# Attention's row maxima subtracted by PE in PSUM, one exp per step, and stage 2's x tile laid over x2

## The chip, the cores and the metric

The kernel runs on one core of a Trainium2 chip. The metric is the device time of one execution in microseconds (us). Engines: PE (TensorE, with its weight loads as PEld), DVE (VectorE), ACT (ScalarE), POOL (GpSimd), SP (SyncE, here a queue of DMA issues).

## What is computed

Three layers run one after the other: attention with banded masks, a mixture of experts whose tokens are assigned one expert each, and a second mixture in which every token goes through all eight experts and the results are weighed by a Sinkhorn-normalised matrix.

```python
def _attn_ref(q, k, v):                      # (4, 8, 576, 64) each
    scores = scale * np.matmul(q, k.transpose(0, 1, 3, 2))
    scores = np.where(masks[None], scores, -1e9)
    scores = scores - np.max(scores, axis=-1, keepdims=True)
    attn = np.exp(scores)
    attn = attn / (np.sum(attn, axis=-1, keepdims=True) + 1e-09)
    return np.matmul(attn, v)
...
    # _moe_ref: one expert per token, 288 tokens per expert
    h = np.maximum(x[mask] @ w1[e], 0.0)
    out[mask] = h @ w2[e]
...
    # _moe2_ref: P from 8 Sinkhorn rounds, every token through every expert
    out += P[:, e:e + 1] * (np.maximum(x @ w1[e], 0.0) @ w2[e])
```

## The kernel before

Each engine takes its instructions in the order in which they are written (the schedule is manual); semaphores join the engines. Three parts matter here.

**Attention** (`attention`, lines 99 to 366). The 4 batches are cut into 6 blocks of 96 queries with 128 keys each. A *unit* has 8 heads: 4 heads of the plain mask (kind 0) and 4 of the dilated one (kind 1, its tokens reordered so that the mask is a band too), one block apart. There are 25 units; the first and the last have one kind only, so half the work. A unit goes through these helpers:

- `scores` (line 163): PE adds the masks as a bf16 product with an identity (line 169, 256 columns, four of them) and Q times K in f32 (line 176, eight products of 128 columns with 64 rows each) into one PSUM tile `ps_s` of two banks; there are two such tiles.
- `row_max` (line 179): DVE reduces `ps_s` to a maximum per row and head (`nm`, line 182), ACT scales it by -1/8 (line 183).
- `exps` (line 186): ACT takes exp of one head at a time, 8 instructions of 128 columns, with the maximum as a bias (line 192). It is a generator: after 4 heads it gives way to `x_out`.
- `p_trans` (line 195): PE transposes the 8 blocks in f32 into `ps_p`, of which there is one.
- `p_evac` (line 203): DVE copies them to SBUF (`pt`, line 207).
- `pv` (line 209): PE multiplies by V (line 218) into `ps_v`, of which there is one; DVE divides by the sums (lines 224 to 226). For some steps PE also makes the router's logits of finished tiles there (line 288) or turns a block (line 258).
- `x_out` (line 237): ACT and POOL split the result into two f16 halves (lines 240, 241), SP stores them.

The loop (line 303) runs 27 iterations. Iteration n writes `scores` and `row_max` of unit n, `p_trans` and `p_evac` of n-1, the exps of n around `x_out` of n-3, and `pv` of n-2. From iteration 4 on, `next(side)` adds half a weight piece of the second mixture's first expert: one ACT instruction (line 742) and one DVE instruction (line 744). `FILL` puts four 512-column products of zeros into iteration 0.

**Stage 1** (`Moe.stage1`) runs routing and the first mixture, and the second mixture's expert 0. It ends with `m2_l1(8)` (line 848, which reads the activations `x2` and the weights `w0h`, `w0l`) and `m2_l2(8)` (line 936), beside the Sinkhorn rounds (lines 1259 to 1270, whose PE product is line 1265: `mean` times `P`, f32, 144 columns).

**Stage 2** (`Moe.stage2`) runs experts 1 to 7 in blocks of 384 tokens. `x_load` (line 1051) brings a block's activations (`xb`, two DMAs of 1344 KB, one buffer), `s_l1` (line 1120) and `s_l2` (line 1158) are its matmuls. Its three SBUF pools are opened in the order `n_t`, `n_x` (the tile `xb`), `n_h`, and lie from address 135200 of a partition upwards, where stage 1's right-hand pools lay until then: `x2h` 137760 to 156192, `x2l` to 174624, the first layer's weights `w0h`, `w0l` to 191008, the second layer's weights to 207392. With this order `xb` lies at 164384 to 185888, over the end of `x2l`, `w0h` and part of `w0l`. The first DMA into it waits for the PE count that the last matmul of line 936 in `m2_l2(8)` brings. Six warming products of 512 columns (line 757) follow `x_load(0)` on PE.

Of the kernel before, what the change touches and what calls it, by code (L numbers as in the profile page):

```python
# [11 lines left out]
F32 = mybir.dt.float32  # L12
F16 = mybir.dt.float16
BF = mybir.dt.bfloat16
I32 = mybir.dt.int32
AF = mybir.ActivationFunctionType
OP = mybir.AluOpType
# [6 lines left out]
QB = 96  # L24
# [7 lines left out]
SC = 0.125  # L32
# [49 lines left out]
NU = len(UNITS)  # L82
# [29 lines left out]
def attention(tc, q, k, v, masks, wg, ident, xd, L, zero, side, early, keep, tables):  # L112

    nc = tc.nc
    with ExitStack() as ctx:
        one = ctx.enter_context(tc.tile_pool(name="a_one", bufs=1))
        ld = ctx.enter_context(tc.tile_pool(name="a_ld", bufs=2))
        vp = ctx.enter_context(tc.tile_pool(name="a_v", bufs=3))
        wk = ctx.enter_context(tc.tile_pool(name="a_w", bufs=2))
        ps = ctx.enter_context(tc.tile_pool(name="a_ps", bufs=2, space=bass.MemoryType.PSUM))  # L120

        raw, T, VR, SS, PP, PT, XT = {}, {}, {}, {}, {}, {}, {}
# [9 lines left out]
        def part(u, size):  # L132

            ks = list(UNITS[u])
            return slice(ks[0] * size // 2, (ks[-1] + 1) * size // 2)

        idf = one.tile([128, 128], F32)
        idb = one.tile([QB, QB], BF)
        idh = one.tile([QB, QB], F16)
        mk = one.tile([QB, MASKS.shape[1], 2, 128], BF)  # L140
        wgf = one.tile([128, 4, E], F32)
        wgh = one.tile([128, 4, E], F16)
# [15 lines left out]
        def op_ap(nm, h, b, j):  # L158
            pair, s = divmod(h, 2)
            p0, n = (max(QB * j - 32, 0), 128) if nm == "k" else (QB * j, QB)  # L160
            return raw[nm, b, pair // 2][64 * s:64 * s + 64, pair % 2, p0:p0 + n]

        def scores(u):
            p = SS[u] = ps.tile([QB, 2, 4, 128], F32, name="ps_s")
            kinds = UNITS[u]
            gs = part(u, 4)
            for s in range(2):
                for n, (kind, (b, j)) in enumerate(kinds.items()):
                    nc.tensor.matmul(p[:, s, 2 * kind:2 * kind + 2, :], idb,
                                     mk[:, MASK_ID[j], kind:kind + 1, :].to_broadcast([QB, 2, 128]),  # L170
                                     start=(n == 0), stop=False, skip_group_check=True)
            for g in range(gs.start, gs.stop):
                for s in range(2):
                    h = 2 * g + s
                    b, j = kinds[g // 2]
                    nc.tensor.matmul(p[:, s, g, :], op_ap("q", h, b, j), op_ap("k", h, b, j), start=False,  # L176
                                     stop=(g + 1 == gs.stop), skip_group_check=True)

        def row_max(u):
            p, gs = SS[u], part(u, 4)  # L180
            nm = wk.tile([QB, 2, 4], F32, name="nm")
            nc.vector.tensor_reduce(nm[:, :, gs], p[:, :, gs], axis=AX.X, op=OP.max)
            nc.scalar.activation(nm[:, :, gs], nm[:, :, gs], AF.Copy, scale=-SC)
            PP[u] = nm

        def exps(u):
            p, nm, gs = SS.pop(u), PP[u], part(u, 4)
            e = wk.tile([QB, 2, 4, 128], F32, name="e")
            PP[u] = e
            for s in range(2):  # L190
                for g in range(gs.start, gs.stop):
                    nc.scalar.activation(e[:, s, g, :], p[:, s, g, :], AF.Exp, bias=nm[:, s, g:g + 1], scale=SC)
                yield

        def p_trans(u):
            e, gs = PP.pop(u), part(u, 4)
            p = ps.tile([128, 2, 512], F32, name="ps_p", bufs=1)
            for s in range(2):
                for g in range(gs.start, gs.stop):
                    nc.tensor.transpose(p[:, s, g * QB:(g + 1) * QB], e[:, s, g, :], idf[:QB, :QB])  # L200
            return p

        def p_evac(u, p):
            gs = part(u, 4)
            t = PT[u] = wk.tile([128, 2, 4, QB], F32, name="pt")
            pp = p[:, :, :4 * QB].rearrange("p s (g q) -> p s g q", g=4)
            nc.vector.tensor_copy(t[:, :, gs], pp[:, :, gs])

        def pv(u, extra, turn=None):
            t = PT.pop(u)  # L210
# [69 lines left out]
        def logits(p, c):  # L280
# [9 lines left out]
            return lambda: nc.vector.tensor_copy(L[:, c, :], p)  # L290

        warm(18)
        nc.vector.tensor_copy(idb, idf[:QB, :QB])
        nc.vector.tensor_copy(idh, idf[:QB, :QB])
        loaded = []
        for kind in (1, 0):
            for nm in "kq":
# [2 lines left out]
            load_v(1, kind)  # L300
        xl = [one.tile([128, 2, 2, S], F16, name="xl%d" % kind) for kind in range(2)]
        first = S * (B - 1) // 128
        for n in range(NU + 2):
            if n < NU:
                scores(n)
                row_max(n)
            if 1 <= n <= NU:
                p_evac(n - 1, p_trans(n - 1))
            ex = exps(n) if n < NU else iter(())
            next(ex, None)  # L310
            if 3 <= n <= NU:
                x_out(n - 3)
            for _ in ex:
                pass
            if n == NU:
                early()
            if n in FILL:
                warm(FILL[n])
            if n >= 2:
                pv(n - 2, [loaded.pop(0)[1] for _ in range(1 if n < NU else 3) if loaded and loaded[0][0] <= n],  # L320
                   n - 3 if NU - 4 <= n <= NU else None)
            if n == 1:
                nc.gpsimd.dma_start(wgf, wg)
                tables()
            elif n == 4:
                nc.scalar.activation(wgh, wgf, AF.Copy, scale=SG)
                nc.vector.scalar_tensor_tensor(wgl, wgf, SG, wgh, op0=OP.mult, op1=OP.subtract)
            if 4 <= n:
                next(side, None)
            if n == 9:  # L330
                tables(True)
            b, c = divmod(n - NJ - 2, NJ)
            if 0 <= b < B - 2 and c < 2:
                load_v(b + 2, 1 - c)
            b, c = divmod(n - NJ, NJ)
            if 0 <= b < B - 2 and c < 2:
                for nm in "kq":
                    load_qk(nm, b + 2, 1 - c)
            b, c = divmod(n - 10, NJ)
            if 0 <= b < B - 1 and c < 3:  # L340
                c0, c1 = S * b // 128, S * (b + 1) // 128
                c0, c1 = c0 + 2 * c, min(c0 + 2 * c + 2, c1)
                if c1 > c0:
                    x_load(c0, c1)
                    loaded += [(n + 3, i) for i in range(c0, c1)]
            if n == NU - 1:
                x_load(first, first + 1)
            if n == NU:
                loaded += [(n, i) for i in (first, first + 1)]
# [5 lines left out]
        p = ps.tile([128, 2, 512], F32, name="ps_v", bufs=1)  # L355
# [311 lines left out]
class Moe:  # L667
# [82 lines left out]
    def psum(self):  # L750
        return self.ps.tile([128, 512], F32, name="mm", bufs=6)

    def warm(self, n):

        p = self.psum()
        for _ in range(n):
            self.nc.tensor.matmul(p, self.zero[:, :128], self.zero, start=True, stop=True)

    def weights(self, key, fetch):

# [608 lines left out]
    def stage2(self, ctx):  # L1369


        pool = lambda n, b: ctx.enter_context(self.tc.tile_pool(name=n, bufs=b))
        self.tp, self.bp, self.hp = pool("n_t", 1), pool("n_x", 1), pool("n_h", 1)

        def part():
            lo = self.tp.tile([128, 2, 2, BLK], F32, name="r", bufs=2).bitcast(F16).rearrange(
                "p a b m -> p (a b m)")[:, :7 * 256].rearrange("p (k c) -> p k c", k=7)
            return self.tp.tile([128, 3, BLK], F32, name="S", bufs=1)[:, :, :256], lo

        def l1(e, n, b):  # L1380
            for j, ns in enumerate(self.s_l1(b)):
                if n and e + 1 < E and j in (0, 1, 3):
                    next(new)
                yield ns

        self.x_load(0)
        for _ in range(6):
            self.warm(1)
        for e in range(1, E):
            order = list(range(NB))[::1 if e % 2 else -1]  # L1390
            new = self.staged(e + 1, part) if e + 1 < E else iter(())
            for n, b in enumerate(order):
                if n == 0:
                    next(new, None)
                interleave(l1(e, n, b), self.side if (e, n) == (1, 0) else None)
                if n + 1 < NB:
                    self.x_load(order[n + 1])
                elif e + 1 < E:
                    self.last_piece()
                    self.w_load(0)  # L1400
                for j, _ in enumerate(self.s_l2(e)):
                    if j in (8, 10, 16, 20, 23, 43):
                        next(new, None)
                if n + 1 == NB:
                    for _ in new:
                        pass
                    if e + 1 < E:
                        self.w_load(1)
# [45 lines left out]
```

## Time and profile before

| what | us |
|---|---|
| three runs | 1804.84, 1805.51, 1808.44 (median 1805.51) |
| the profiled execution, its own time | 1803.2 |
| its span | 1801.4 |
| PE busy | 1738.0 (96% of the span) |
| DVE busy | 1359.0 (75%) |
| ACT busy | 852.7 (47%) |
| POOL busy | 239.6 (13%) |
| mean granted clock of TensorE | 0.982 of full speed |

The span is what the profile records; the execution's own time has 1.8 us around it. Attention takes about the first 115 us, stage 1 lasts until about 629 us, stage 2 until the end. "Busy" on PE is modelled, since matmuls are pipelined: an instruction's duration includes its way through the array, so the pace of a stream is read from the starts, or from the chain of waits, where consecutive pieces stand end to end.

### The profile page before, as it was taken

How to read it: one execution, taken by the hardware profiler on the slowest of the kernel's cores; microseconds unless marked ns; L12 is line 12 of the kernel's file. 1: busy time of each engine (PE TensorE's matmuls, PEld its weight loads, DVE VectorE, ACT ScalarE, POOL GpSimd, SP SyncE). 2: the span in 40 equal slices, each digit the busy share in tenths (PEclk: the TensorE clock that was granted, in tenths of full speed). 3: DMA queues.
4: the chain of work that ended last, by engine and by line, in shares of the span. 5: the costliest groups of instructions: out<-in, count | busy, mean ns of one | idle time of the engine just before them, and what ended most of it. 6: DMA issues, size and time to landing. Idle time of an engine off the chain costs nothing.

```text
span 1801.4 us, 35276 instructions
## 1 busy us (share of the span) xinstructions
PE 1738.0 (96%) x14464; PEld 1290.0 (72%) x14464; DVE 1359.0 (75%) x2583; ACT 852.7 (47%) x1581; POOL 239.6 (13%) x297
## 2 busy tenths in 40 slices
PE   9986899999999989999999999999999999999998
PEld 7864676667776657777777777777777777777776
DVE  6977785678744858878887888788788878887556
ACT  5853442343443345555554456444455544464433
POOL 2423331223320000000000000000000000000111
PEclk9977999999999999999999999999999999999999
DMA  8923441424442132445225443424452254433020
GB/s 295 288 65 108 121 121 61 131 78 121 143 139 67 57 130 98 170 154 201 114 89 206 159 150 133 162 101 170 157 197 116 90 202 159 150 134 154 36 97 36
DMA packets 105554, 241.20 MB, mean 134 GB/s; under 512 B 46192, under 2 KB 69888, under 8 KB 98480
## 3 DMA queue, kind: packets, MB, share of 16 engines
q1 hardware_dynamic: 84592, 151.27, 24.3%
q0 software_dynamic: 20544, 87.42, 13.8%
q8 instruction: 113, 1.85, 0.4%
q14 instruction: 49, 0.40, 0.1%
q10 hardware_dynamic: 256, 0.26, 0.0%
HBM read 173.63 MB, written 61.73 MB: 131 GB/s over the span
## 4 chain that ended last, share of the span: by engine, by line
PE 72%; DVE 11%; issue 10%; ACT 4%; DMA 2%; POOL 1%; SPq 0%; POOLq 0%; ACTq 0%; DVEq 0%
PE mm L1120 27%; PE mm L1158 23%; PE mm L848 8%; PE mm L936 5%; PE mm L892 2%; PE r L542 1%; PE ps_v L218 1%; DVE hl L1077 1%; PE ps_p L200 1%; PE ps_s L176 1%; POOL out_dram L1172 1%; DVE G L488 1%; DVE w1l L789 1%; DVE G L615 1%; ACT w1h L788 1%
## 5 line engine op out<-in xcount | busy, mean ns | idle before, releaser
L1120 PE MATMUL mm<-xb,w1h 128*128 128x384 f16 x2352 | 574.8, 327 | 7.8 <-issue 4.8
L1158 PE MATMUL mm<-w2h,hh 128*128 128x256 f16 x1764 | 480.8, 273 | 0.4
L1158 PE MATMUL mm<-w2h,hl 128*128 128x256 f16 x1764 | 480.8, 273 | 0.0
L1158 PE MATMUL mm<-w2l,hh 128*128 128x256 f16 x1764 | 480.8, 273 | 0.0
L1120 PE MATMUL mm<-xb,w1l 128*128 128x384 f16 x1176 | 383.9, 326 | 0.0
L1158 PEld LDWEIGHTS <-hh 128*128 128x128 f16 x3528 | 345.2, 98 | 43.1 <-issue 0.9
L1120 PEld LDWEIGHTS <-w1h 128*128 128x128 f16 x2352 | 230.3, 98 | 159.5 <-issue 11.4
L1158 PEld LDWEIGHTS <-hl 128*128 128x128 f16 x1764 | 172.6, 98 | 19.9
L1077 DVE TENSOR_TENSOR hl<-r,hh 128x1536 f16<-128x1536 f32 x84 | 147.5, 1756 | 42.7 <-ACT hh L1076 42.7
L1120 PEld LDWEIGHTS <-w1l 128*128 128x128 f16 x1176 | 115.2, 98 | 79.3 <-issue 3.5
L1072 ACT ACTIVATE r<-mm 128x384 f32<-128x384 f32 x252 | 119.1, 481 | 100.0 <-PE mm L1120 100.0
L1038 POOL DMA_DIRECT2D ws<-raw x48 | 26.1, 543 | 944.1 <-ACT raw L989 532.3
L1076 ACT ACTIVATE hh<-r 128x1536 f16<-128x1536 f32 x84 | 124.6, 1483 | 43.6 <-DVE r L1101 41.6
L1083 ACT ACTIVATE mm<-mm 128x384 f32<-128x384 f32 x84 | 40.3, 479 | 185.0 <-PE mm L1120 185.0
L1077 DVE TENSOR_TENSOR hl<-S,hh 128x1152 f16<-128x1152 f32 x84 | 113.6, 1352 | 0.0
L1168 DVE SCALAR_TENSOR_TENSOR acc<-t,P,acc 128x512 f32<-128x512 f32 x126 | 94.7, 752 | 4.5
L848 PE MATMUL mm<-xt,w1h 128*128 128x288 f16 x512 | 95.9, 286 | 1.7 <-DVE xt L865 1.7
L1076 ACT ACTIVATE hh<-S 128x1152 f16<-128x1152 f32 x84 | 96.3, 1147 | 0.0
L854 DVE SCALAR_TENSOR_TENSOR w1l<-mm,w1h 128x288 f16<-128x288 f32 (+1 forms) x120 | 50.3, 437 | 60.4 <-ACT w1h L853 59.8
L989 ACT ACTIVATE raw<-raw 128x1024 f16<-128x1024 f32 x48 | 50.6, 1055 | 87.3 <-DVE raw L973 45.5
L853 ACT ACTIVATE w1h<-mm 128x288 f16<-128x288 f32 (+1 forms) x120 | 46.9, 395 | 80.9 <-PE mm L848 78.4
L848 PE MATMUL mm<-x2l,w0h 128*128 128x256 f16 x288 | 79.9, 278 | 3.8 <-DVE x2l L897 3.8
(271 smaller groups left out, 2973.4 us busy)
## 6 DMA issues: line engine op xcount, KB each, us to landing
xb<-xw SPq DMA_DIRECT2D x30, 1344.0 KB, 8.7
ws<-raw POOLq DMA_DIRECT2D x48, 448.0 KB, 3.9
ws<-r POOLq DMA_DIRECT2D x48, 448.0 KB, 3.1
raw<-in_w2b_dram SPq DMA_DIRECT2D x32, 512.0 KB, 4.1
raw<-in_w1b_dram SPq DMA_DIRECT2D x56, 256.0 KB, 9.1
w1h<-ws SPq DMA_DIRECT2D x6, 1792.0 KB
w1l<-ws SPq DMA_DIRECT2D x6, 1792.0 KB
w2h<-ws SPq DMA_DIRECT2D x6, 1792.0 KB
```

Of the source, the lines that this page charges most:

```text
L848: nc.tensor.matmul(p, a[:, k, 128 * f:128 * (f + 1)], rhs(k, b), start=(done[f] == 1 and i == 0), stop=(done[f] == KT and i == 2), skip_gr ...
L853: nc.scalar.activation(h[0][:, f, :n], p, AF.Relu)
L854: nc.vector.scalar_tensor_tensor(h[1][:, f, :n], p, 0.0, h[0][:, f, :n], op0=OP.max, op1=OP.subtract)
L936: nc.tensor.matmul(p, a[:, f, c], b[:, f, :], start=(f == 0 and n == 0), stop=(f == FT - 1 and n == 2))
L989: self.nc.scalar.activation(hi[:, k], x, AF.Copy, scale=sw)
L1072: nc.scalar.activation(o, p, AF.Relu, scale=SH)
L1076: yield nc.scalar.activation(hq[0][:, i, k], x, AF.Copy)
L1077: yield V.tensor_sub(hq[1][:, i, k], x, hq[0][:, i, k])
L1083: nc.scalar.activation(Q[i], P[i], AF.Copy)
L1120: nc.tensor.matmul(p, w[u][:, 2 * j + i // 2, k, 128 * (i % 2):128 * (i % 2 + 1)], x[:, v, r, j], start=(q in (1, 5) and j == 0 and n == 0 ...
L1158: nc.tensor.matmul(p, h[u][:, i, a, 128 * t:128 * (t + 1)], w[v][:, i, b, :], start=(q in (1, 7) and i == 0 and j == 0), stop=(q in (2, 3) ...
L1168: V.scalar_tensor_tensor(self.acc[:, r, :], x, self.P[:, r, e:e + 1], self.acc[:, r, :], op0=OP.mult, op1=OP.add)
```

## The change

- The maxima no longer go to ACT as a bias. A new helper, `less_max`, lets PE add `neg` (minus the identity, f32, in place of an unused f16 identity) times `nm` to the scores that stand in PSUM: one f32 product for each of the two banks, `nm` broadcast along the 128 keys of a head, so 512 columns (256 in the first and the last unit). The scaling of `nm` on ACT goes.
- `exps` is one instruction for all 8 heads, 1024 columns, with no bias.
- `p_evac` runs on ACT instead of DVE.
- `scores` and `row_max` of unit n+1 are written in iteration n, behind `less_max(n)` and `exps(n)`.
- Stage 2 opens `n_x` ahead of `n_t`, so `xb` lies at 135200 to 156704, over `x2h` and 512 bytes of `x2l`. In the built program its first DMA now waits for the PE count of the last matmul of `m2_l1(8)`. Its place in SP's queue is the same.
- The warming products ahead of stage 2 are three, of 1, 1 and 512 columns.

```diff
-        idh = one.tile([QB, QB], F16)
+        neg = one.tile([QB, QB], F32, name="neg")
...
             nc.vector.tensor_reduce(nm[:, :, gs], p[:, :, gs], axis=AX.X, op=OP.max)
-            nc.scalar.activation(nm[:, :, gs], nm[:, :, gs], AF.Copy, scale=-SC)
             PP[u] = nm
 
+        def less_max(u):
+            p, nm, gs = SS[u], PP[u], part(u, 4)
+            for s in range(2):
+                nc.tensor.matmul(p[:, s, gs, :], neg, nm[:, s, gs].unsqueeze(2).to_broadcast([QB, gs.stop - gs.start, 128]),
+                                 start=False, stop=True, skip_group_check=True)
+
         def exps(u):
-            p, nm, gs = SS.pop(u), PP[u], part(u, 4)
-            e = wk.tile([QB, 2, 4, 128], F32, name="e")
-            PP[u] = e
-            for s in range(2):
-                for g in range(gs.start, gs.stop):
-                    nc.scalar.activation(e[:, s, g, :], p[:, s, g, :], AF.Exp, bias=nm[:, s, g:g + 1], scale=SC)
-                yield
+            p, gs = SS.pop(u), part(u, 4)
+            e = PP[u] = wk.tile([QB, 2, 4, 128], F32, name="e")
+            nc.scalar.activation(e[:, :, gs], p[:, :, gs], AF.Exp, scale=SC)
...
-            nc.vector.tensor_copy(t[:, :, gs], pp[:, :, gs])
+            nc.scalar.activation(t[:, :, gs], pp[:, :, gs], AF.Copy)
...
-        nc.vector.tensor_copy(idh, idf[:QB, :QB])
+        nc.vector.tensor_scalar(neg, idf[:QB, :QB], -1.0, None, op0=OP.mult)
...
+        scores(0)
+        row_max(0)
         for n in range(NU + 2):
             if n < NU:
-                scores(n)
-                row_max(n)
+                less_max(n)
+                exps(n)
+            if n + 1 < NU:
+                scores(n + 1)
+                row_max(n + 1)
             if 1 <= n <= NU:
                 p_evac(n - 1, p_trans(n - 1))
-            ex = exps(n) if n < NU else iter(())
-            next(ex, None)
             if 3 <= n <= NU:
                 x_out(n - 3)
-            for _ in ex:
-                pass
...
-    def warm(self, n):
+    def warm(self, n, width=512):
 
-        p = self.psum()
+        p = self.psum()[:, :width]
         for _ in range(n):
-            self.nc.tensor.matmul(p, self.zero[:, :128], self.zero, start=True, stop=True)
+            self.nc.tensor.matmul(p, self.zero[:, :128], self.zero[:, :width], start=True, stop=True)
...
-        self.tp, self.bp, self.hp = pool("n_t", 1), pool("n_x", 1), pool("n_h", 1)
+        self.bp, self.tp, self.hp = pool("n_x", 1), pool("n_t", 1), pool("n_h", 1)
...
         self.x_load(0)
-        for _ in range(6):
-            self.warm(1)
+        for n in 1, 1, 512:
+            self.warm(1, n)
```

Line numbers move a little: `less_max` is line 188 of the changed kernel, the exp is line 194 (before 192), 200, 207, 218 and 240 become 201, 208, 219 and 241, and from line 742 on two are added (848 is 850, 936 is 938, 1051 is 1053, 1120 is 1122).

On PE, one iteration of attention before, from its masks to P times V (a row with x4 or x8 is so many instructions; an f32 product that isn't a transpose stands in the trace as two records):

```order
L169 MATMUL ps_s<-mk,idb 96x256
L176 MATMUL ps_s<-rawk_143,rawq_145 96x128 x4
L176 MATMUL ps_s<-rawk_137,rawq_139 96x128 x4
L200 MATMUL ps_p<-idf,e 128x96 x8
L218 MATMUL ps_v<-rawv_149,pt 96x65 x4
L218 MATMUL ps_v<-rawv_147,pt 96x65 x4
```

The same stretch of PE's order in the changed kernel, with the numbers of the tiles:

```order
L188 MATMUL ps_s_253<-nm_266,neg_132 96x512 x2
...
L169 MATMUL ps_s_293<-mk_133,idb_131 96x256
L176 MATMUL ps_s_293<-rawk0_143,rawq0_145 96x128 x4
L176 MATMUL ps_s_293<-rawk1_137,rawq1_139 96x128 x4
L201 MATMUL ps_p_308<-idf_130,e_251 128x96 x8
L219 MATMUL ps_v_323<-rawv0_149,pt_277 96x65 x4
L219 MATMUL ps_v_323<-rawv1_147,pt_277 96x65 x4
L188 MATMUL ps_s_293<-nm_306,neg_132 96x512 x2
```

The two products of line 188 are new, and they close the tile (`ps_s_253`) whose scores were written an iteration earlier; the next unit's scores (`ps_s_293`) follow, and its own line 188 stands behind the transposes and P times V.

On ACT, one iteration of attention before, and the same in the changed kernel:

```order
L183 ACTIVATE nm<-nm 96x8
L192 ACTIVATE e<-ps_s,nm 96x128 x4
L240 ACTIVATE xo<-xt 96x2x256
L192 ACTIVATE e<-ps_s,nm 96x128 x4
L742 ACTIVATE w0h<-raw 128x512
```

```order
L194 ACTIVATE e<-ps_s 96x1024
L208 ACTIVATE pt<-ps_p 128x768
L241 ACTIVATE xo<-xt 96x2x256
L744 ACTIVATE w0h<-raw 128x512
L194 ACTIVATE e<-ps_s 96x1024
```

Nine exps and scalings have become one exp, and the copy of P stands where the second half of the exps stood.

## Rows read from the trace of the kernel before

**Rows 1.** The page: busy time of each engine; the granted clock in 40 slices.
```profile
PE 1738.0 (96%) x14464; PEld 1290.0 (72%) x14464; DVE 1359.0 (75%) x2583; ACT 852.7 (47%) x1581; POOL 239.6 (13%) x297
...
PEclk9977999999999999999999999999999999999999
```
**Rows 2.** Busy time by stretch: length, PE, PEld, DVE, ACT, POOL, clock, DMA share, GB/s.
```profile
45.00:60.00 15.00, 15.00 (x176) 13.26 (x175) 14.36 (x25) 13.39 (x45) 7.83 (x10) 1.00 1.02 310
```
**Rows 3.** Chain of waits in attention: start us, us on the chain, what.
```profile
18.32 0.44 PE ps_s L169 x4
18.75 1.05 PE ps_s L176 x16
19.80 0.81 PE ps_p L200 x8
20.61 1.33 PE ps_v L218 x16
...
60.25 0.28 PE ps_v L288 x12
```
**Rows 4.** PE in order of time: start, us, instruction, [idle before, releaser].
```profile
21.78 0.60 PE L169 MATMUL ps_s<-mk,idb 96*96 96x256 bf16 x4
...
103.68 0.38 PE L169 MATMUL ps_s<-mk,idb 96*96 96x256 bf16 x2
...
110.75 1.57 PE L218 MATMUL ps_v<-rawv,pt 128*96 128x65 f32 x16 [0.88 <-ACT x L234]
...
113.46 1.44 PE L218 MATMUL ps_s<-rawv,pt 128*96 128x65 f32 x8
```
**Rows 5.** PE and DVE in order of time, at the start of attention.
```profile
12.51 1.12 PE L176 MATMUL ps_s<-rawk,rawq 64*96 64x128 f32 x16 [1.71 <-DMA rawq<-in_q_dram]
...
13.66 1.22 DVE L182 TENSOR_REDUCE nm<-ps_s 96x8 f32<-96x1024 f32 x1 [3.54 <-PE ps_s L176]
```
**Rows 6.** Chain of waits at the end of stage 1, two pieces.
```profile
599.84 3.24 PE mm L936 x15
...
627.81 0.24 PE r L1265 x2
```
**Rows 7.** Groups of ACT and DVE, 20 to 100 us; last row: the page's.
```profile
L192 ACT ACTIVATE e<-ps_s,nm 96x128 f32<-96x128 f32 x156 | 44.1, 366 | 0.7
L240 ACT ACTIVATE xo<-xt 96x512 f16<-96x512 f32 (+1 forms) x20 | 12.4, 620 | 0.0
L742 ACT ACTIVATE w0h<-raw 128x512 f16<-128x512 f32 x8 | 5.2, 650 | 0.0
...
L182 DVE TENSOR_REDUCE nm<-ps_s 96x8 f32<-96x1024 f32 x20 | 24.3, 1214 | 1.4 <-PE ps_s L176 1.4
L207 DVE COPY pt<-ps_p 128x768 f32<-128x768 f32 x20 | 18.9, 944 | 0.2 <-PE ps_p L200 0.2
...
L989 ACT ACTIVATE raw<-raw 128x1024 f16<-128x1024 f32 x48 | 50.6, 1055 | 87.3 <-DVE raw L973 45.5
```
**Rows 8.** Chain of waits across the border of stage 1 and stage 2.
```profile
628.71 0.23 PE mm L757
...
629.13 8.71 DMA xb<-xw
...
637.88 1.76 PE mm L1120 x5
...
640.12 10.01 PE mm L1120 x57
```
**Rows 9.** SP's queue, 580 to 640 us: who waited for whom, us, times, longest.
```profile
SPq L1051 <- PE mm L757: 24.5, 1, 24.5
```
**Rows 10.** PE and DVE in order of time: last line-848 matmul; last P.
```profile
614.68 0.27 PE L848 MATMUL mm<-x2l,w0h 128*128 128x256 f16 x1
...
630.51 0.31 DVE L1262 TENSOR_TENSOR P<-P,rs 128x144 f32<-128x144 f32 x1
```
**Rows 11.** Busy time by stretch, as rows 2, behind the load.
```profile
640.00:641.00 1.00, 1.00 (x5) 0.48 (x4) 0.74 (x4) 0.21 (x1) 0.00 (x0) 0.50 0.00 0
```

## The prediction

> **What bounds the kernel now.** The page's first part comes first: PE is busy for 96% of the span, every other engine much less, and the line of granted clocks is at full speed except in its third and fourth slices [rows 1]. A share over the whole run says little about one stage, so next come the two places that the change touches.
>
> The first is attention, about 8 to 114 us. Between 45 and 60 us PE is busy for all 15 us, but DVE for 14.4 and ACT for 13.4 [rows 2]: three engines are close together, and only the chain tells which of them sets the pace. It stays on PE, piece after piece: 0.44 (mask) + 1.05 (scores) + 0.81 (transposes) + 1.33 (P times V) = 3.63 us for an undisturbed step; logits for one tile add 0.28 to 0.30 [rows 3]. Iteration 4 starts on PE at 21.78 and iteration 24 at 103.68 [rows 4]: 20 steps in 81.9 us. Their work is 20 x 3.63 = 72.6, nine logit groups 2.7 and ten turned blocks of about 0.09, 0.9, so 5.7 us of these 20 steps is waiting. From 12.51, when K and Q have landed [rows 5], to 21.78 it is another 1.2 by the same sum, and from 103.68 to the end of the last P times V (it starts at 113.46 and is through at about 114.6) about 4.4, with the wait of 0.88 us for ACT in it [rows 4]. **PE therefore has 11.3 us of slack in 102 us**, and no more. Whatever is put on PE above that lengthens the stage.
>
> The second place is the border between the stages. The queue of SP waits for PE with the load of stage 2's x tile [rows 9], the load goes out at 629, runs 8.71 us, and PE starts line 1120 at 637.88 [rows 8]; then it runs at half clock until about 641.5 [rows 11].
>
> **Off ACT and DVE.** Eight exps per step cost ACT 44.1 x 8/156 = 2.26 us [rows 7]. One exp of 1024 columns I put at 1.06, from line 989, which has as many [rows 7]; the scaling of the maxima (about 0.2) goes and the copy of P comes, bounded by 0.62 (512 columns, line 240) and 1.06, say 0.82. With xo at 0.62 and a weight half at 0.65, ACT comes to about 3.2 us a step. DVE, which has about 3.8 us a step, 96% of the time [rows 2], loses the copy, 0.94 [rows 7]. What hides this is PE: both engines were already below its pace, so these savings count only inside the 11.3 us.
>
> **Onto PE.** less_max issues two f32 products a step, 512 columns each, 256 in the first and last steps. No row shows a moving operand that is broadcast along its columns. The nearest is sinkhorn's f32 product, 144 columns in two records, 0.24 us [rows 6]: 1.67 ns a column, so 0.853 us for 512. Fifteen f16 products of 512 columns take 3.24 us, 0.216 each [rows 6], so f32 costs four times that. Cheaper bounds: the transposes, 768 f32 columns in 0.81 us, and the scores, 1024 in 1.05 [rows 3], both about 0.53 for 512; and the masks in bf16, 0.44 for 1024 columns [rows 3], 0.22 for 512. I take 0.853: the sinkhorn row is the same kind of operation on the full array in f32, where the scores use half of the rows each and the transposes are another mode. So 23 x 1.71 + 2 x 0.85 = 41.0 us, of which the first 0.85 lies under the wait for K and Q. An upper end: four weight loads that are not covered, up to 0.05 us a step, 1.2 in all; I add 0.6. **Added on PE: 40.7.**
>
> **What waits now.** In the new order a step is less_max(n), scores(n+1), transposes(n-1), P times V(n-2), 5.4 us. The maximum of n is taken under 0.81 + 1.33 us of PE work and needs 1.2 [rows 7]: covered. exp(n) and the copy of P have a whole step. If DVE is late by a weight half, the cover goes (a rival below). Remaining waits: the four warm products move from the wait for K and Q to behind scores(1), 0.85 (as 4 x 0.216); less_max(1) waits for its maximum until 14.95 [rows 5], 0.4; in step 2 only four transposes lie in between, 0.9; at the tail P times V(23) still waits for ACT's copies, about 1.2. Sum 3.4. So **attention: +40.7 - 11.3 + 3.4 = +32.8**, say 33. The bounds are 28 (the stalls go wholly) and 38 (half of the slack stays). The routing behind it is the same chain of work, only later, and I cost its shift at nothing; no load that it waits for is issued earlier or later against it.
>
> **Stage 2's x tile.** In the built program the load waits for the PE count that the last matmul of m2_l2(8) reached; after the change, for that of the last matmul of m2_l1(8), the last reader of x2. That one starts at 614.68 [rows 10]. Nothing else holds SP's queue: it had been standing at this load for 24.5 us [rows 9], since 604. 614.95 + 0.8 for two issues + 8.71 is 624.5: under the remaining stage 1 matmuls, which end at 628.71 [rows 8], with 4 us to spare. PE then goes on after one 512-column warm and two of one column, about 629.1. What is late next is sinkhorn: its product behind the first group of line 1120 needs P, which DVE finishes at 630.82 [rows 10], so PE stands still for about 0.7 us and is through that product at 631.1 instead of 640.12 [rows 8]: 9.0 us. From 640.12 to 641.5 line 1120 ran at half clock [rows 11], which costs 0.7 us that is not paid if PE never stops. **-9.7**, bounds -8 (the clock falls in the short stop anyway, or the queue is slower) and -10.5.
>
> **The sum.** 33 - 9.7 = +23.3. The profiled execution took 1803.2, so 1826.5 for one like it; the median of the runs shown is 2.3 us above it, 1805.5, and 1805.5 + 23.3 gives **1828.8**; I forecast 1828.5.
>
> **Rivals.**
> *f32 is cheaper here.* If the broadcast products went at the pace of the scores, 0.525, PE gets 24.7 instead of 40.1: -11.3 + 3.4 + 0.6 gives +17.4, less 9.7 is +7.7, 1813. For it: scores and transposes are f32 and run at that pace. Against it: the sinkhorn row. Chance 0.09. The Trainium skill, Trace Analysis, Engine Utilization, has f32 (as low and high parts) at half of the matmul rate: 0.43 us for 512 columns would make it about 1809. It also says, TensorE: Matmul & The Clock Gate, Back-to-back issue gap, that a sustained stream of 512-column products is spaced 131 ns: four passes would then be 0.52, the same 1813. The rows of this trace speak against both, 0.24 us for 144 f32 columns and 0.216 for 512 in f16 [rows 6].
>
> *Faster: the broadcast operand streams at the pace of bf16.* In less_max all 128 columns of a group are one word; if PE took them at the masks' 0.22 for 512 columns, it gets 10.3, and with -11.3 + 4.0 attention is +3; less 9.7 the kernel is at 1799. It decides once a 512-column product is below 0.35 us (17 us over the 24 steps, which is 9.7 plus the slack that is used), 0.69 ns a column against the 1.67 of [rows 6]. No row supports it. Chance 0.04.
>
> *The cover of the maxima breaks.* DVE works on a weight half when scores(n+1) is done; row_max starts later and less_max, with all of PE's queue behind it, waits up to 0.5 us in the 16 steps that have one: +8, 1837. Against: the new step leaves DVE over 2 us idle. Chance 0.06.
>
> *The x tile isn't early after all*, because something else holds SP's queue or the tile: +33 alone, 1838. Against: the count in the built program. Chance 0.03.
>
> **How the numbers follow.** Forecast 0.78 (its own bounds, 28 - 8 to 38 - 10.5 turned round, reach from 1823 to 1836). To leave out no more than 2 in 10, the range takes in the pace of the scores and the broken cover: 1813 to 1837. A measurement of this kernel can tell about 0.2%, 3.6 us, from no change: faster means below 1801.9. Faster 0.05 (the bf16 pace and a little beside it), same 0.03 (between the two cheap cases), slower 0.92.
>
> **What would show it.** In the changed profile: line 188 (less_max), 100 records of f32, about 0.43 us each in the chain and 41 us in all; iterations of attention 5.4 us apart with PE alone on the chain; ACT at some 60% and DVE at some 55% there; attention's end about 33 us later; x's load issued as the last line-850 matmul ends, landed before line 938 ends, and no stretch at half clock behind it. It is wrong if line 188's records take 0.3 us or less, if iterations are under 4.7 us, or if the load still goes out behind the last line-938 matmul.

## The result and the profile after

The changed kernel takes 1831.25 us (median of four runs, 1829.30 to 1832.71), the kernel before 1806.97 beside it: a ratio of 1.0136, 95% interval 1.0116 to 1.0156. The forecast was 1828.5 in a range of 1813 to 1837, and 0.92 for slower: slower it is, by 24.3 us where 23.3 were worked out. Two of its terms can be read apart from each other in the profile, which is of the run of 1832.71. That run lies 1.5 us above its median and the profiled run of before, 1803.2, lies 3.8 below its own, so the two profiles differ by some 5 us more than the medians do.

The page of the changed kernel, the rows that answer to [rows 1]:

```profile
PE 1773.7 (97%) x14561; PEld 1303.5 (71%) x14561; DVE 1335.7 (73%) x2558; ACT 839.3 (46%) x1414; POOL 230.4 (13%) x297
...
PEclk9996899999999999999999999999999999999999
```

PE's busy time grew by 35.7 us, DVE's and ACT's fell by 23 and 13; the span grew from 1801.4 to 1830.8.

The chain of waits in attention, one iteration (start us, us on the chain, what), which answers to [rows 3]:

```profile
37.43 1.75 PE ps_s L188 x4
39.18 0.44 PE ps_s L169 x4
39.62 1.05 PE ps_s L176 x16
40.66 0.81 PE ps_p L201 x8
41.48 1.33 PE ps_v L219 x16
42.81 1.75 PE ps_s L188 x4
```

Mask, scores, transposes and P times V take what they took, 3.63 us; line 188 stands in front with 1.75, and nothing else is on the chain: 5.38 us a step. Its four records are two products of 512 columns, so one product costs 0.875.

Busy time in a stretch of attention (columns as in [rows 2]):

```profile
80.00:100.00 20.00, 20.00 (x198) 14.40 (x198) 10.51 (x22) 10.23 (x16) 4.61 (x4) 1.00 0.94 263
```

DVE and ACT, at 96% and 89% in [rows 2], are now busy for half of the time. The relief is real, but nothing waits for it.

PE in order of time at the tail of attention (start, us, instruction, [idle before, releaser]), which answers to the last two of [rows 4]:

```profile
144.72 1.57 PE L219 MATMUL ps_v<-rawv,pt 128*96 128x65 f32 x16 [0.43 <-ACT x L235]
...
148.51 1.57 PE L219 MATMUL ps_v<-rawv,pt 128*96 128x65 f32 x16 [1.21 <-ACT x L235]
...
150.89 1.28 PE L219 MATMUL ps_s<-rawv,pt 128*96 128x65 f32 x8
```

The last P times V starts at 150.89 instead of 113.46: attention is 37.4 us longer in this execution.

At the border the load goes out at the end of the last line-850 matmul. First the waits of SP's queue (us, times, longest), then SP's own order of time, then the chain, each of the changed kernel; they answer to [rows 9] and [rows 8]:

```profile
SPq L1053 <- PE mm L850: 10.5, 1, 10.5
```

```profile
653.77 0.82 SPq L1053 DMA_DIRECT2D xb<-xw  x2
```

```profile
669.73 0.48 PE r L1267 x2
670.21 19.82 PE mm L1122 x122
```

The DMA is off the chain. PE waits for P instead and has sinkhorn's product behind it at 670.21. Busy time there (columns as in [rows 2]):

```profile
668.00:670.00 2.00, 0.99 (x7) 0.50 (x6) 1.41 (x6) 0.58 (x2) 0.00 (x0) 1.00 0.00 0
```

PE idles for a microsecond and the clock stays at its upper level, 2.4 GHz, where [rows 11] has 0.50. The last matmul that reads x2 starts at this time:

```profile
653.47 0.27 PE L850 MATMUL mm<-x2l,w0h 128*128 128x256 f16 x1
```

So from there to the stretch of line 1122 behind sinkhorn's product it is 16.74 us; before it was 640.12 - 614.68 = 25.44 [rows 8, 10], so 8.7 are saved. The rest of the span, from 670.21, is 1160.6 against 1161.3: another 0.7, which fits the half clock of [rows 11] (it is 1161.4 in e2, which has that stretch, and 1160.6 in e1 and 1161.1 in e10, which have none behind the load). The spans differ by 29.4: +37.4 in attention, -8.7 and -0.7 at the border, and +1.4 between them, in code that the change doesn't touch (501.2 us before; 499.9 to 501.2 in e1 to e4).

### The profile page after: what moved, and what is told of

Its sections match the earlier page's. It is cut to its first block, busy times and chain, and to the rows that moved or that the text cites. A ratio compares the mean times of both kernels' runs of the same rounds, so it can differ in the third digit from the quotient of the medians.

```text
span 1830.8 us, 35253 instructions
## 1 busy us (share of the span) xinstructions
PE 1773.7 (97%) x14561; PEld 1303.5 (71%) x14561; DVE 1335.7 (73%) x2558; ACT 839.3 (46%) x1414; POOL 230.4 (13%) x297
## 4 chain that ended last, share of the span: by engine, by line
PE 75%; issue 10%; DVE 9%; ACT 3%; DMA 1%; POOL 1%; SPq 0%; POOLq 0%; ACTq 0%; DVEq 0%
PE mm L1122 27%; PE mm L1160 24%; PE mm L850 8%; PE mm L938 4%; PE ps_s L188 2%; PE mm L894 2%; PE ps_v L219 2%; PE ps_s L176 1%; PE r L544 1%; PE ps_p L201 1%; POOL out_dram L1174 1%; DVE G L490 1%; DVE w1l L791 1%; DVE G L617 1%; ACT w1h L790 1%
## 5 line engine op out<-in xcount | busy, mean ns | idle before, releaser
L1079 DVE TENSOR_TENSOR hl<-S,hh 128x1152 f16<-128x1152 f32 x84 | 113.5, 1351 | 0.0
## 6 DMA issues: line engine op xcount, KB each, us to landing
raw<-in_w2b_dram SPq DMA_DIRECT2D x32, 512.0 KB, 10.4
```

The source lines that it names most:

```text
L1079: yield V.tensor_sub(hq[1][:, i, k], x, hq[0][:, i, k])
```

## The experiments

Each kernel was timed beside the kernel before on one chip. e5 to e8 ran on another chip than e1 to e4, on which before takes 1821.8 us, and e9 and e10 on a further one (1806.4), so ratios are compared across them, and times of whole runs only within a group. (A ratio is not exactly that of the two medians.)

### e1: the stage 2 part alone

```diff
 # before.py
...
-        self.tp, self.bp, self.hp = pool("n_t", 1), pool("n_x", 1), pool("n_h", 1)
+        self.bp, self.tp, self.hp = pool("n_x", 1), pool("n_t", 1), pool("n_h", 1)
...
-        for _ in range(6):
-            self.warm(1)
+        for n in 1, 1, 512:
+            self.warm(1, n)
```

> Before with the stage 2 part alone (x tile over x2, three warming products of 1, 1 and 512 columns). Theory: the load goes out as the last line-848 matmul of stage 1 ends, some 14 us ahead of where it went before, lands under stage 1's last matmuls, and the kernel takes 9 to 10 us less than before (about 1796 to 1797), with no stretch at half clock at the border. Rival (the load only moves its wait elsewhere, or the earlier transfer slows something beside it): less than 3 us of gain.

Measured: 1794.97 us beside 1805.37, ratio 0.9943 (0.9927 to 0.9959), 10.4 us faster. SP's queue, waits of e1:

```profile
SPq L1051 <- PE mm L848: 10.5, 1, 10.5
```

The load waits for line 848 and no longer for the end of stage 1. The profile of e1 has one stretch below full clock at the border, though, against the expectation:

```profile
622.00:628.00 6.00, 6.00 (x24) 2.69 (x23) 4.56 (x13) 2.01 (x3) 0.00 (x0) 0.79 0.12 43
```

PE had waited there for DVE, 2.3 us in all between 617 and 621. The changed kernel has the same wait and stayed at full clock in its profile, as did e8 and e10, so this part of the expectation holds in some executions only. It costs 1.3 us (18.0 us from the last reader of x2, at 612.76, to the stretch of line 1120 at 630.78, against 16.7).

### e2: attention alone

```diff
 # after.py
...
-        self.bp, self.tp, self.hp = pool("n_x", 1), pool("n_t", 1), pool("n_h", 1)
+        self.tp, self.bp, self.hp = pool("n_t", 1), pool("n_x", 1), pool("n_h", 1)
...
-        for n in 1, 1, 512:
-            self.warm(1, n)
+        for _ in range(6):
+            self.warm(1)
```

> The changed kernel without the stage 2 part. Theory: attention alone costs 33 to 38 us (about 1839 to 1845), and the border of the stages shows the same 8.7 us load and half clock as before. Rival (the two parts act on each other, for instance the later end of attention shifts what the border waits for): more than 4 us away from the sum of the changed kernel and the gain of e1.

Measured: 1840.41 us, ratio 1.0194 (1.0169 to 1.0219), 35.0 us slower. The two parts add up: 0.9943 x 1.0194 = 1.0136, the ratio of the changed kernel. The chain of e2 at the border is that of before:

```profile
664.76 8.51 DMA xb<-xw
673.27 0.04 issue
673.32 1.76 PE mm L1122 x5
```

### e3: neg and the maxima in bf16

```diff
 # after.py
-        neg = one.tile([QB, QB], F32, name="neg")
+        neg = one.tile([QB, QB], BF, name="neg")
...
-            nm = wk.tile([QB, 2, 4], F32, name="nm")
+            nm = wk.tile([QB, 2, 4], BF, name="nm")
```

> The changed kernel with neg and the maxima in bf16: the subtraction is two bf16 products of 512 columns a step; the maximum is rounded, which the division by the sum takes out again. Theory (the f32 price of line 188 is the cause): a 512-column product takes 0.22 us, line 188 0.44 a step in place of 1.75, iterations 4.1 us apart in place of 5.4, attention about 30 us shorter than in the changed kernel, the whole at 1799 to 1803, a little faster than before. Rival (the new order, the single exp or the copy on ACT set the step): iterations stay above 4.8 us and the kernel above 1815.

Measured: 1800.49 us, ratio 0.9972 (0.9960 to 0.9983). The chain of e3, one iteration:

```profile
26.72 0.43 PE ps_s L188 x2
27.15 0.44 PE ps_s L169 x4
27.59 1.05 PE ps_s L176 x16
28.64 0.81 PE ps_p L201 x8
29.45 1.33 PE ps_v L219 x16
30.78 0.43 PE ps_s L188 x2
```

Only line 188 has changed, from 1.75 to 0.43, and the iteration from 5.38 to 4.06. Order, single exp and copy on ACT are the same in both, so none of them lengthens the step; the f32 product does. The last P times V starts at 120.2, still 6.7 us behind before: even 0.43 us a step, 8.7 in 20 steps, is more than the 5.7 us that 20 steps of before waited. (Its first steps ran partly at half clock too, 0.66 in 12 to 17 us, and the tail still waits.)

### e4: the warming products back in the wait for K and Q

```diff
 # after.py
         scores(0)
         row_max(0)
+        warm(4)
         for n in range(NU + 2):
...
-            if n in FILL:
-                warm(FILL[n])
```

> The changed kernel with the four warming products of iteration 0 put ahead of less_max(0), into the wait for K and Q, where they stood before. Theory (with no work in that wait the granted clock fell to half at 12 to 17 us, which made scores(1), the warming products and less_max(1) take 6.4 us instead of some 3.7): full clock there, attention ends about 3 to 4 us earlier than in the changed kernel (0.9 of it because the products no longer stand in the path). Rival (the clock falls there whatever PE does, as the load is late): half clock still in 12 to 17 us and at most 1 us gained.

Measured: 1829.67 us in one run. At full clock from 12 to 17 us, as theory has it, but this settles little, as the profiles of the changed kernel and of e2 show. Their attention is the same code. PE in the changed kernel:

```profile
12.44 2.03 PE L176 MATMUL ps_s<-rawk,rawq 64*96 64x128 f32 x16 [0.39 <-DMA rawq<-in_q_dram]
14.39 1.89 PE L156 MATMUL ps_v<-zero 128*128 128x512 f16 x4
16.07 2.81 PE L188 MATMUL ps_s<-nm,neg 96*96 96x512 f32 x4
```

PE in e2:

```profile
12.41 1.12 PE L176 MATMUL ps_s<-rawk,rawq 64*96 64x128 f32 x16 [0.46 <-DMA rawq<-in_q_dram]
13.46 1.04 PE L156 MATMUL ps_v<-zero 128*128 128x512 f16 x4
14.85 1.96 PE L188 MATMUL ps_s<-nm,neg 96*96 96x512 f32 x4 [0.34 <-DVE nm L182]
```

Busy time of the changed kernel, and then of e2, in that stretch:

```profile
12.00:17.00 5.00, 4.62 (x23) 2.73 (x23) 1.22 (x1) 0.02 (x1) 0.00 (x0) 0.50 1.02 423
```

```profile
12.00:17.00 5.00, 4.24 (x28) 2.27 (x28) 1.22 (x1) 0.48 (x2) 0.00 (x0) 1.00 1.01 421
```

The same instructions ran at 1.2 GHz in one execution and at 2.4 in the other. e10, with before's attention and the products in the wait, has 0.66 there. So whether the clock falls at the start changes from execution to execution, and the place of the products does not decide it. In e4 less_max(1) starts at 14.97, in e2 at 14.85: with full clock moving the products gained nothing, since less_max(1) waits for its maximum until then, and the last P times V starts at 149.3, 0.2 behind e2's. Both halves of the expectation (the cause, and the 0.9 us) fall.

### e5: the order alone

```diff
 # before.py
+        scores(0)
+        row_max(0)
         for n in range(NU + 2):
-            if n < NU:
-                scores(n)
-                row_max(n)
+            ex = exps(n) if n < NU else iter(())
+            next(ex, None)
+            if n + 1 < NU:
+                scores(n + 1)
+                row_max(n + 1)
             if 1 <= n <= NU:
                 p_evac(n - 1, p_trans(n - 1))
-            ex = exps(n) if n < NU else iter(())
-            next(ex, None)
```

> Before with one thing changed: scores and row_max of unit n+1 are written in iteration n, behind the first four exps of n. Eight exps with a bias, the scaling of the maxima on ACT and the copy of P on DVE stay, stage 2 as before. Theory (PE's work sets the step, and the order alone can only give back PE's waits, of which ACT at 3.75 and DVE at 3.8 us a step leave little): iterations of 3.8 to 4.0 us, the kernel within 5 us of before, on either side. Rival (the order itself makes the changed kernel's steps long, as a maximum is now waited for on PE's or ACT's queue): iterations above 4.4 us and more than 10 us slower than before.

Measured: 1844.87 us beside 1821.8, ratio 1.0114 (1.0086 to 1.0141). The rival's numbers came true. The chain of e5:

```profile
66.59 0.60 PE ps_s L169 x4
67.19 1.07 PE ps_s L176 x16
...
68.36 1.23 DVE nm L182
...
69.75 0.19 ACT xo L240
...
70.29 1.12 ACT e L192 x4
...
71.45 0.60 PE ps_s L169 x4
```

It is a ring of 4.86 us over three engines. On ACT the scaling of the maxima of n+1 now stands between the two halves of the exps of n, so the second half waits for scores(n+1) and row_max(n+1); and scores(n+2) waits for that second half, which frees one of the two `ps_s` tiles. The changed kernel has the order without the ring, since no ACT instruction waits for row_max there. One more scores tile was not tried, so this cause of the ring is read from the chain and not tested.

### e6: one maximum for the eight heads of a row, no products of line 188

```diff
 # after.py
-            nm = wk.tile([QB, 2, 4], F32, name="nm")
-            nc.vector.tensor_reduce(nm[:, :, gs], p[:, :, gs], axis=AX.X, op=OP.max)
+            nm = wk.tile([QB, 1], F32, name="nm")
+            nc.vector.tensor_reduce(nm, p[:, :, gs].rearrange("p s g c -> p s (g c)"), axis=AX.XY, op=OP.max)
+            nc.vector.tensor_scalar(nm, nm, -SC, None, op0=OP.mult)
...
-            nc.scalar.activation(e[:, :, gs], p[:, :, gs], AF.Exp, scale=SC)
+            nc.scalar.activation(e[:, :, gs], p[:, :, gs], AF.Exp, bias=nm, scale=SC)
...
-                less_max(n)
```

> The changed kernel with no products of line 188: DVE takes one maximum over all eight heads of a row, scales it, and the single exp takes it as its bias (softmax does not depend on which constant is taken off; rows whose heads lie far apart would underflow sooner). Theory (only what stands on PE counts, and the slack in the waits is worth 7 to 9 us once ACT and DVE are relieved): iterations of 3.65 to 3.75 us, the last P times V starts at 105 to 108 us instead of 113.5 before, and with stage 2's 9.5 us the kernel takes 1787 to 1791, the fastest of all. Rival (with less_max gone ACT or DVE sets the step): iterations above 3.9 us, 1794 or more.

Measured: 1814.29 us beside 1821.8, ratio 0.9948 (0.9928 to 0.9968): 7.5 us faster than before by the medians (9.5 by the ratio), where theory had 14 to 18. Its iterations are 3.63 us where nothing interferes, so ACT and DVE do not bound. The chain leaves PE elsewhere:

```profile
77.66 8.34 DMA xT<-xd
...
86.50 0.48 PE ps_s L169 x4
86.97 1.45 PE ps_s L176 x16
88.42 1.48 PE ps_p L196 x8
```

The faster PE reaches the logits of a tile, three iterations after its transposing load was written, before the load has landed (it waits for such loads twice, 1.9 us). After that wait the scores take 1.45 us instead of 1.05; the granted clock is 0.50 from 88 to 90. The last P times V starts at 114.8, against 117.5 in e8, before's attention on the same chip.

As a whole, though, e6 is no faster than e8 (1810.58 in one run). The 2.7 us are lost behind attention: PE waits longer there for `xt`, the tokens of the first mixture's first expert, in e6 and then in e8:

```profile
PE mm L844 <- ACT xt L863: 8.0, 1, 8.0
```

```profile
PE mm L848 <- ACT xt L867: 4.5, 1, 4.5
```

The same wait is 8.2 us in e5 and 8.5 in e7, and 0.8 to 1.8 in all the other profiles. What sets it no run shows, so from e5 to e8 the steps of attention and the border are compared, and whether e6's form pays as a whole is left to e9 and e10.

### e7: the copy of P back on DVE

```diff
 # after.py
-            nc.scalar.activation(t[:, :, gs], pp[:, :, gs], AF.Copy)
+            nc.vector.tensor_copy(t[:, :, gs], pp[:, :, gs])
```

> The changed kernel with the copy of P back on DVE. Theory (PE alone sets the step, so where the copy runs is worth nothing): iterations still 5.38 us apart, the last P times V within 1.5 us of e2's 149.1, the kernel within 4 us of the changed kernel. Rival (ACT's copy is part of what lengthens the step): iterations below 5.2 us.

Measured: 1845.65 us in one run, 1.0131 of that chip's 1821.8, as the changed kernel's 1.0136. (The expectation's "within 4 us of the changed kernel" can be held only as a ratio, since the chip is another.) The chain of e7:

```profile
62.01 1.75 PE ps_s L188 x4
...
67.39 1.75 PE ps_s L188 x4
```

5.38 us again, and the last P times V at 148.9 (e2: 149.1). Where the copy runs is worth nothing while PE sets the step.

### e8: the pool order without the dropped warming products

```diff
 # before.py
-        self.tp, self.bp, self.hp = pool("n_t", 1), pool("n_x", 1), pool("n_h", 1)
+        self.bp, self.tp, self.hp = pool("n_x", 1), pool("n_t", 1), pool("n_h", 1)
```

> Before with the order of stage 2's pools alone: x tile over x2, six warming products of 512 columns as before. Theory (the pool order is the whole gain of the stage 2 part; the products it drops would stand in the path now, but PE waits for sinkhorn's P behind them in any case): the load goes out with the last line-848 matmul, PE ends sinkhorn's product at the border 0 to 1 us later than in e1, the kernel 8 to 10 us faster than before. Rival (the warming products matter): 2 us or more behind e1 at the border.

Measured: 1810.58 us in one run, 0.9938 of 1821.8. The chain of e8 at the border:

```profile
642.53 1.29 PE mm L757 x6
643.83 0.97 PE mm L1120 x6
644.80 0.41 PE r L1265 x2
645.21 4.88 PE mm L1120 x30
```

Six products take 1.29 us and end where PE would otherwise wait for P: sinkhorn's product follows without a gap. From the last reader of x2 to 645.21 it is 16.7 us, as in the changed kernel. The pool order is the whole gain at the border.

### e9 and e10: a version that beats both, and its measure

e9 is e6 with these lines; e10 is the kernel of e1 again, on the same chip.

```diff
 # e6
+        warm(4)
         for n in range(NU + 2):
...
-            if n in FILL:
-                warm(FILL[n])
...
-                    loaded += [(n + 3, i) for i in range(c0, c1)]
+                    loaded += [(n + 4, i) for i in range(c0, c1)]
```

> e6 with two things changed: the logits of a tile of x come four iterations after its load is issued instead of three, and the four warming products of iteration 0 stand in the wait for K and Q. Theory (in e6 the steps became so short that the transposing loads of x came late, 1.6 us and 1.4 us of direct wait and a fall of the clock behind it): PE no longer waits for these loads, the last P times V starts 5 us or more before that of e10 on the same chip, and the kernel is 0.2 to 0.4% faster than e10. Rival (the loads of the first 80 us, at a DMA share near 1.0, bound attention whatever PE does): the last P times V within 3 us of e10's, the kernel within 0.2% of it.

> The same kernel as e1 (before with the stage 2 part alone), once more, on the chip of e9, so that the two can be compared: 0.5 to 0.65% faster than before.

Measured: e9 1791.63 us, ratio 0.9922 (0.9908 to 0.9937); e10 1797.93, ratio 0.9957 (0.9943 to 0.9971); before 1806.42. e9 is 6.3 us, 0.35%, faster than e10 by their medians, and e10 confirms e1 within the intervals (a little under the stated 0.5%). The chain of e9, and the start of its last P times V:

```profile
34.00 0.44 PE ps_s L169 x4
...
37.63 0.44 PE ps_s L169 x4
```

```profile
107.06 1.44 PE L214 MATMUL ps_s<-rawv,pt 128*96 128x65 f32 x8
```

Steps of 3.63 us, no wait of PE for the transposing loads, and attention ends 9.2 us ahead of e10 (116.24); up to 2 us of that may be the granted clock at 12 to 17 us, 1.00 in e9 and 0.66 in e10. The two changes over e6 were made together, and their shares were not measured apart. Most of the waiting that is left sits at the tail, where P times V waits for ACT's copy of the turned block, 2.8 us in all. By its ratio e9 is the fastest kernel of the study: DVE and ACT relieved as in the change, nothing added on PE, and the x tile early.

## Why the prediction was right, point by point

- **PE bounds attention, with 11.3 us of slack.** Right in kind. The steps between e9, e3 and the changed kernel are 3.63, 4.06 and 5.38 us while line 188 takes 0, 0.43 and 1.75: what is added on PE appears in full in the step. As a size, 11.3 belongs to one execution: the last P times V of before's attention starts between 112.9 (e1) and 117.5 (e8).
- **Off ACT and DVE: it counts only inside the slack.** Right: in e7, with the copy of P back on DVE, the step is still 5.38. The single exp took 1.02 us and the copy 0.81 (1.06 and 0.82 were put); both engines are busy for just over half of the time.
- **0.853 us for an f32 product of 512 columns.** 0.875 measured, 2.4% more, and the two cheaper prices from [rows 3] are out. bf16 products of the same width and the same broadcast operand take 0.217 in e3, as much as the f16 products of [rows 6] with no broadcast (0.216), so the broadcast neither helps nor hurts, and f32 costs four times. The upper end for the weight loads, 0.05 us a step, had no row behind it; the steady step came within it, 0.04 above the bare price (1.75 against 1.71). The Trainium skill's half rate for f32 as low and high parts (Perfetto Trace Analysis, Engine Utilization) and its 131 ns for a sustained 512-column product (TensorE: Matmul & The Clock Gate, Back-to-back issue gap) are not what a product costs in these runs: 0.875 and 0.217. Half the rate holds for each of the two records of an f32 product, 0.4375.
- **What waits now: 3.4 us.** The steps at the start came as worked out: scores(2) end at about 18.3 in e2, and less_max(2) starts at 19.61 behind its maximum. The tail was set at 1.2, and that was too little: P times V alone waits 0.43 + 1.21.
- **Attention +33.** This is the term that was mis-sized: +35.6 in e2, at full clock (149.1 against 113.5), and +37.4 in the profile of the changed kernel, whose start ran at half clock and lost another 2 us (less_max(1) at 16.07, and scores(2) 2.1 us later than in e2). The prediction had no term for a fall of the clock there. The other 2.6 us are, as far as e2's chain tells, two terms. Line 188 takes 41.9 us there, 1.2 above the 40.7 that were put (its first three steps took 1.96, 1.96 and 1.82). And the slack did not go wholly. From the masks of unit 24 to the last P times V it is 12.26 us, against 9.78 before, with 3.7 us of work added in between, so of the 4.4 us of waiting at before's tail about 3.2 are left, not 1.2. Together the two come to 3.2, a little more than the miss.
- **x tile: -9.7.** 8.7 and 0.7 in the profile, 9.4; e1 10.4 +- 3 and e10 8.5 +- 2.5 by the runs. The load landed under stage 1's last matmuls, sinkhorn's P was what PE waited for next, as written, and the half clock went. Its chance of not being early fell to nothing in e1.
- **The sum.** +35.6 - 9.4 = 26.2 by terms, 24.3 measured as medians. By the medians of e2 and e1 the parts are +35.0 and -10.4, 24.6 together: attention was put 2 us too low and the border's gain 0.7 too low, and the second hides part of the first. That the sum came within 1 us is in part luck; the range would have held the miss in attention as well.
- **Rivals.** *f32 is cheaper* and *faster at bf16's pace* fell with the chain's 1.75. *The cover of the maxima breaks* did not happen in the steady steps: line 188 follows P times V without a gap.

## What to carry to other kernels

Relieving engines that stand just below the bound is worth only what the bounding engine waits for, so count that first: here 11 us in 102, from the chain's undisturbed step against the measured distance of two steps; and not all of it is given back, as the waits at the tail show. Before work is moved onto the bound, look for a type that costs a quarter, or for a form that needs none of it: one maximum over all heads did the same service as a bias (with it, rows whose heads lie far apart underflow sooner). A tile's place in memory decides what its first load waits for; laying it over what dies first took 9 us off the border, and e6 and e9 show that shortening one engine's steps can call for moving the uses of loads a step later as well.

## What was not expected

- The granted clock at 12 to 17 us was 1.00 in before, e2, e4, e7 and e9, 0.66 in e1, e3, e6, e8 and e10, 0.70 in e5 and 0.50 in the changed kernel. The changed kernel and e2 have the same attention code, so it varies between executions; between these two it is worth about 2 us.
- With the order one step ahead and the biased exps kept (e5), three engines formed a ring of 4.86 us a step although PE's own work is 3.63 and ACT's and DVE's about 3.8: the two score tiles tie ACT's second half of the exps to PE's next scores.
- In e6 attention became bound by the transposing loads, which no view of before shows as a wait of PE: there they have 3 steps of 3.6 to 4.1 us, and in e6 3.63 was too little with a DMA share near 1.0.
